# Score matmuls in two pairs per step, each into the two PSUM banks that one min pass leaves

## The chip, the core and the metric

The kernel runs on one NeuronCore of a Trainium2 chip. The metric is the device time of one execution in microseconds (us). Engines are named as the profile names them: PE (TensorE matmuls), PEld (its weight loads), DVE (VectorE), ACT (ScalarE), POOL (GpSimd), SP (the queue that issues most DMAs). Each engine takes its instructions in order and waits on semaphores for the others.

## The reference

Threshold attention over 8 batches x 8 heads x 576 positions with head size 64, followed by a hash-routed mixture of 8 experts over the 4608 resulting rows of 512. All of it is float32.

```python
scores = (1 / 8) * q @ k.T                       # per batch and head, 576 x 576
thresh = max(scores, axis=-1) - tau
scores = where(scores >= thresh, scores, -1e9)
attn   = exp(scores - max(scores)); attn /= sum(attn) + 1e-9
x      = (attn @ v), laid out as (4608, 512)
e      = token_ids * 2654435761 % 8              # the expert of each row
out    = relu(x @ w1[e]) @ w2[e]
```

## The kernel before

**Attention** takes two heads of one batch at a time, a *pair* `p`, 32 pairs in all. The 576 query rows of a head are cut into a tail of 64 and four chunks of 128. A pair is a *block* of five *steps*, `n = 5 p + s`. Step s = 0 is the tails of both heads in one 128-row tile; steps s = 1 to 4 are one 128-row chunk of each head, so they have two score tiles, head j = 0 and j = 1. One score tile is 128 rows x 576 keys in float32, which is two PSUM banks of 288 keys each (i = 0 and 1).

What a step does to a score tile, in the names used below:

- **scores** (`score`, matmuls L202 for s = 0, L209 otherwise): PE writes q k^T to PSUM. A step s >= 1 has four such calls, (i, j) = (0,0), (0,1), (1,0), (1,1). Head 0 uses rows 0 to 63 of the PE array and head 1 rows 64 to 127, so one call of each head can run side by side. Each call shows as two matmul instructions in the profile, eight in a step.
- **min pass** (`negate`, L221): DVE reads the two banks, writes the negated scores `ns` to SBUF and their row minimum `nmx`. POOL then makes the threshold `thr` from it (L225).
- **exp** (`expo`, L232): ACT makes `w = exp(-ns + nmx)`.
- **mask pass** (`mask`, L243): DVE zeroes what is under the threshold and sums the rows. It comes one step later, behind the min passes of step n + 1.
- **turn** (`turn_w`, transposes L254): two steps later PE transposes `w` into the one PSUM tile `tr` (two banks, one buffer), and ACT copies that back to SBUF (`put_wT`, L270 and L275). There are two turns per step, one per head (a tail has one). A turn can't start before the copy of the turn before it has left `tr`.
- **products** (`av_part`, L285): with the transposed weights of the pair before, PE forms w v in the tile `av`, in four parts: two for the first query columns (g = 0, steps 1 and 2) and two for the rest (g = 1, steps 3 and 4). ACT copies `av` out (L301), and in step 0 of the next block PE turns it back (`turn_o`), ACT and DVE scale it by the reciprocal sums (`put_xt` L323, `put_xm` L332) and SP writes it to DRAM.

PSUM has eight banks: two score tiles (the pool `ps_sc`, two rotating buffers of two banks), `tr` and `av`. A score tile of head j of step n + 1 takes over the buffer of the score tile two back in the rotation, so its matmuls wait for that tile's min pass; the first call of head 0 waits for one min pass and the first call of head 1, right behind it in PE's order, for the next.

The order of every engine's work is written out by hand (`manual_schedule`, the loop from L547). For PE the order of a block is:

| step | PE, in order |
|---|---|
| s = 0 | turn_o; first turn; scores of step 1; second turn |
| s = 1 | products g 0, chunks 0 to 2; first turn; scores of step 2; second turn |
| s = 2 | products g 0, chunks 3 and 4; the one turn of the tail; scores of step 3 |
| s = 3 | first turn; products g 1, chunks 0 to 2; second turn; scores of step 4 |
| s = 4 | first turn; products g 1, chunks 3 and 4; second turn; scores of the next step 0 |

DVE has per step: the min passes of step n, then (s = 0) `put_xm`, then the mask passes of step n - 1, then in early blocks a piece of the routing arithmetic, or in s = 2 a reciprocal before its min passes. ACT has in steps 1 and 2 the exp of head 0, the copy of the first turn, the exp of head 1, the copy of the second turn; in steps 3 and 4 the copy of the first turn, both exps, the copy of the second turn. At the start of step 1 POOL scales the next q tile (L182).

**The experts** follow. The router's indices are worked out during the first blocks; during the last ones rows are gathered and the first two experts' weights loaded. The first expert's first product is begun between the last steps (`early_h`, `early_xT`, L488 to L526), and the rest is a loop over the experts of `gemm1` (L651), `gemm2` (L667) and transposes. `gemm1`, `early_h`, `late_h` and `early_xT` take their PSUM from the score pool as well.

Of the kernel before, what the change touches and what calls it, by code (L numbers as in the profile page):

```python
# [20 lines left out]
def kernel(  # L21
# [17 lines left out]
    P = 128  # L39
# [31 lines left out]

    consts = ctx.enter_context(tc.tile_pool(name="consts", bufs=1))
    w_pool = ctx.enter_context(tc.tile_pool(name="w_pool", bufs=2))
    ps_sc = ctx.enter_context(tc.tile_pool(name="ps_sc", bufs=2, space=PSUM))

    ident = consts.tile([P, P], FP32, name="ident")
    u128 = consts.tile([P, P], BF16, name="u128")
# [15 lines left out]
    xT_0 = consts.tile([P, CO, CAP], FP32, name="xT_0")  # L93
    h_0 = consts.tile([P, FO, CAP], FP32, name="h_0")
    w_tiles = {}

    def gather(x_dram, dst, idx):
        nc.gpsimd.indirect_dma_start(
# [19 lines left out]
    with tc.tile_pool(name="a_q", bufs=1) as a_q, \  # L118
# [25 lines left out]

        oT = a_o.tile([P, 64 + S], FP32, name="oT")
        av = ps_av.tile([P, 2, 512], FP32, name="av")
        kts, kxs, rss, recs, scs, nss, stats, ws = {}, {}, {}, {}, {}, {}, {}, {}

        def load_pair(p):
            hp, b = divmod(p, B)  # L150
# [34 lines left out]
        def heads(n):  # L185
            return 1 if n % NS == 0 else 2

        def score(n):


            p, s = divmod(n, NS)
            q_sb, k_sb = q_bufs[p % 3], kts[p]
            for j in range(heads(n)):
                sc = ps_sc.tile([P, 2, 512], FP32, name="sc")
                scs[n, j] = sc
            if s == 0:

                for j in range(2):
                    for i in range(2):
                        rows, cols = slice(64 * i, 64 * i + 64), slice(64 * j, 64 * j + 64)  # L200
                        rhs = k_sb[rows, S2 * i:S2 * i + S2] if i == j else kxs[p][rows, :]
                        nc.tensor.matmul(scs[n, 0][cols, i, 0:S2],  # L202
                                         lhsT=q_sb[rows, TAIL + 64 * j:TAIL + 64 * j + 64],
                                         rhs=rhs, start=True, stop=True)
                return
            for i in range(2):
                for j in range(2):
                    rows, cols = slice(64 * j, 64 * j + 64), slice(P * (s - 1), P * s)
                    nc.tensor.matmul(scs[n, j][:, i, 0:S2], lhsT=q_sb[rows, cols],  # L209
                                     rhs=k_sb[rows, S2 * i:S2 * i + S2], start=True, stop=True)  # L210

        def negate(n):

            nmx = a_st.tile([P, 2], FP32, name="nmx")
            thr = a_st.tile([P, 2], FP32, name="thr")
            stats[n] = (nmx, thr)
            for j in range(heads(n)):
                sc = scs.pop((n, j))
                ns = a_ns.tile([P, S], FP32, name="ns")
                nss[n, j] = ns  # L220
                nc.vector.tensor_scalar(out=ns[:].rearrange("p (i s) -> p i s", i=2),  # L221
                                        in0=sc[:, :, 0:S2], scalar1=-1.0, scalar2=None,
                                        op0=ALU.mult, op1=ALU.min, accum_out=nmx[:, j:j + 1])
            nj = heads(n)
            nc.gpsimd.tensor_scalar(out=thr[:, 0:nj], in0=nmx[:, 0:nj], scalar1=drop[:],  # L225
                                    scalar2=None, op0=ALU.add)

        def expo(n, j):
            c0 = 64 if n % NS == 0 else S * j
# [69 lines left out]
        def put_oT(g):  # L299
            c0, width = ((64, WA), (64 + WA, WB))[g]  # L300
            nc.scalar.copy(oT[:, c0:c0 + width], av[:, g, 0:width])  # L301
# [198 lines left out]
        def early_h():  # L500

            w1_sb = w_tiles[0, 1]
            for fo in range(FO):
                h_ps = ps_sc.tile([P, 2, 512], FP32, name="sc")
                for i in range(2):
                    for co in range(CO - 1):
                        nc.tensor.matmul(h_ps[:, i, 0:CH], lhsT=w1_sb[:, co, fo * P:fo * P + P],
                                         rhs=xT_0[:, co, i * CH:i * CH + CH],
                                         start=(co == 0), stop=(co == CO - 2))
                        if (i, co) == (1, CO - 2):  # L510
                            nc.vector.tensor_copy(
                                h_0[:, fo].rearrange("p (i t) -> p i t", i=2), h_ps[:, :, 0:CH])
                        yield

        def late_h():

            w1_sb = w_tiles.pop((0, 1))
            for fo in range(FO):
                h_ps = ps_sc.tile([P, 2, 512], FP32, name="sc")
                for i in range(2):  # L520
                    nc.tensor.matmul(h_ps[:, i, 0:CH], lhsT=w1_sb[:, CO - 1, fo * P:fo * P + P],
                                     rhs=xT_0[:, CO - 1, i * CH:i * CH + CH], start=True,
                                     stop=True)
                h3 = h_0[:, fo].rearrange("p (i t) -> p i t", i=2)
                nc.vector.tensor_tensor(out=h3, in0=h3, in1=h_ps[:, :, 0:CH], op=ALU.add)
                nc.scalar.activation(h3, h3, AF.Relu)  # L526
# [12 lines left out]
        with tc.manual_schedule():  # L539
# [3 lines left out]
                nc.tensor.transpose(tr[:, 0, 0:P], ident[:], ident[:])  # L543
            next(pieces)
            scale_q(0)
            score(0)
            for n in range(LAST + NS + 1):  # L547
                p, s = divmod(n, NS)
                m = n - 2
                if s == 0 and p + 2 < NP:  # L550
                    load_pair(p + 2)
                if s == 0 and p + 1 < NP:
                    load_v(p + 1)
                if s == 1 and p + 1 < NP:
                    scale_q(p + 1)
                if s == 2 and p in (20, 24):
                    load_w1(p // 4 - 5)
                if s == 2 and p in (22, 26):
                    load_w2((p - 22) // 4)

                q = p - 1
                if s == 1 and 0 <= q < NP:
                    add_eps(q)
                if s == 2 and 0 <= q < NP:
                    nc.vector.reciprocal(recs[q][:], recs[q][:])
                if n == LAST:
                    tr = ps_sc.tile([P, 2, 512], FP32, name="sc")
                    early_xT(tr, 0, 2, 0, CO - 1)
                if s == 0 and p >= 2:
                    turn_o()  # L570
                    put_xt(p - 2)
                if n == LAST:
                    tr = ps_sc.tile([P, 2, 512], FP32, name="sc")
                    early_xT(tr, 2, 4, 0, CO - 1)
                if s in (1, 2) and 0 <= q < NP and n != LAST + 1:
                    av_part(q, 0, ((0, 1, 2), (3, 4))[s - 1])
                if n < LAST and s in (1, 2):
                    negate(n)
                    expo(n, 0)
                if s == 2 and 0 <= q < NP:  # L580
                    put_oT(0)
                if n > LAST:
                    fill(1)
                turned = 0 <= m < LAST
                if turned:
                    tr = turn_w(m, 0)
                    put_wT(m, 0, tr)
                if n == LAST:
                    tr = ps_sc.tile([P, 2, 512], FP32, name="sc")
                    early_xT(tr, 4, 5, 0, CO - 1)  # L590
                    put_xm(p - 2)
                    av_part(q, 0, (0, 1, 2))
                if n >= LAST:
                    fill(1)
                if s in (3, 4) and 0 <= q < NP:
                    av_part(q, 1, ((0, 1, 2), (3, 4))[s - 3])
                if n < LAST and s not in (1, 2):
                    negate(n)
                    expo(n, 0)
                if s == 0 and p >= 2 and n != LAST:  # L600
                    put_xm(p - 2)
                if s == 4 and 0 <= q < NP:
                    put_oT(1)
                if n < LAST and heads(n) == 2:
                    expo(n, 1)
                if s in (0, 1, 2) and n + 1 < LAST:
                    score(n + 1)
                if turned and heads(m) == 2:
                    tr = turn_w(m, 1)
                    put_wT(m, 1, tr)  # L610
                if s in (3, 4) and n + 1 < LAST:
                    score(n + 1)
                if 0 < n <= LAST:
                    for j in range(heads(n - 1)):
                        mask(n - 1, j)
                next(pieces, None)


                g = n - G0
                if 0 <= g < 2 * KT:  # L620
                    fetch(g // KT, g % KT, 0)
                if n == LAST:
                    fill(1)
# [8 lines left out]
    with tc.tile_pool(name="m_x", bufs=1) as m_x, \  # L632
# [17 lines left out]

        def gemm1(w1_sb, xT, h_sb, n, width):  # L651
            for fo in range(FO):
                h_ps = ps_sc.tile([P, 2, 512], FP32, name="sc")
                for i in range(n):
                    for co in range(CO):
                        nc.tensor.matmul(h_ps[:, i, 0:width],  # L656
# [94 lines left out]
```

## Time and profile before

| | |
|---|---|
| median of 11 runs | 1077.1 us (1073.16 to 1080.24) |
| the profiled execution | 1077.27 us, its span 1075.6 us |
| first to last min pass (attention) | 12.4 to 499.2 us from the span's start |
| last products and first expert's start | to about 535 us |
| experts, PE without a pause worth telling | from there to the end |
| granted PE clock, 100 to 500 us | 1.00 |
| busy in 100 to 500 us (400 us) | PE 390.2, PEld 259.9, DVE 373.9, ACT 340.7, POOL 137.2 us |
| one block, tail min pass to tail min pass | 15.08 to 15.09 us in 18 of the 23 blocks 8 to 30; 15.2 to 17.3 in blocks 1 to 7; 14.75 in 26 and 27 |

How to read it: all times are us from the span's start. In the timeline a row is a run of like instructions, with its start, the time from its first start to its last end, and in brackets how long the engine was idle before it and who ended that. Starts of matmuls stand closer than their durations: a run of eight score matmuls without a wait takes 1.19 to 1.20 us though each lasts 0.40 to 0.46, since two run side by side and each pair starts before the last has ended. So a PE that is busy in the table can still have been waiting. In the experts' part PE sets the pace; in the attention PE, DVE and ACT take turns at it.

### The profile page before, as it was taken

The page shows a single profiled execution, that of the slowest core. Times are in us where ns is not written, and L with a number is a line of the kernel's source. Part 1 is how long each engine was busy: PE and PEld are TensorE (multiplying, and loading weights), DVE is VectorE, ACT ScalarE, POOL GpSimd, SP SyncE. Part 2 cuts the span into 40 slices and gives each one's busy share as a digit, 9 for nine tenths or more (in the row PEclk, how much of TensorE's full clock was granted, in tenths as well). Part 3 has the DMA queues.
Part 4 walks back from the last instruction along what each step waited for, and adds up shares of the span by engine and source line. Part 5 has one row for each costly group of instructions (what it writes and reads, how often), then busy time and mean ns, then how long its engine had stood idle before and what let it go on. Part 6 is the DMA issues. An engine that isn't in the chain of part 4 may idle for free. (4 is left out here: it accounts for less than half of the span.)

```text
span 1075.6 us, 20177 instructions
## 1 busy us (share of the span) xinstructions
PE 1043.8 (97%) x7438; PEld 650.9 (61%) x7438; DVE 522.9 (49%) x1347; ACT 469.1 (44%) x798; POOL 299.5 (28%) x397
## 2 busy tenths in 40 slices
PE   7999999999999999999999999999999999999996
PEld 5666666666666666666655746557466475564652
DVE  8898899999999999996330100100101001010000
ACT  5788888888888888887020000010000000000000
POOL 2566632222222225422433114022140140101001
PEclk8899999999999999999999999999999999999998
DMA  4332343333335656411133124212242042300000
GB/s 118 93 97 67 97 103 87 84 90 104 97 89 156 177 177 203 124 46 30 36 132 113 53 89 143 87 59 96 96 147 85 30 131 95 103 0 35 9 18 27
DMA packets 95460, 97.40 MB, mean 91 GB/s; under 512 B 33275, under 2 KB 70269, under 8 KB 95362
## 3 DMA queue, kind: packets, MB, share of 16 engines
q1 hardware_dynamic: 87170, 77.20, 24.6%
q0 software_dynamic: 8192, 18.91, 5.2%
q8 instruction: 60, 0.98, 0.4%
q14 instruction: 38, 0.31, 0.1%
HBM read 78.18 MB, written 19.98 MB: 91 GB/s over the span
## 5 line engine op out<-in xcount | busy, mean ns | idle before, releaser
L670 PE MATMUL o_ps<-w_sb,h 128*122 128x512 f32 x640 | 280.6, 592 | 0.0
L232 ACT ACTIVATE w<-ns,nmx 128x576 f32<-128x576 f32 x288 | 220.4, 777 | 35.8 <-DVE ns L221 34.0
L243 DVE SCALAR_TENSOR_TENSOR w<-ns,thr,w 128x576 f32<-128x576 f32 x288 | 232.7, 840 | 0.0
L656 PE MATMUL sc<-xT,w_sb 128*128 128x305 f32 x896 | 231.2, 419 | 0.0
L221 DVE TENSOR_SCALAR_CACHE_REDUCE ns<-sc 128x576 f32<-128x576 f32 x288 | 207.2, 752 | 23.9 <-PE sc L209 22.3
L656 PEld LDWEIGHTS sc<-xT,w_sb 128*128 128x128 f32 x896 | 169.1, 189 | 63.4 <-issue 3.4
L670 PEld LDWEIGHTS o_ps<-w_sb,h 128*122 128x122 f32 x640 | 115.6, 185 | 138.9 <-issue 138.5
L209 PE MATMUL sc<-k_sb,q 64*128 64x288 f32 x1024 | 181.3, 429 | 1.5 <-DVE ns L221 1.5
L254 PEld LDWEIGHTS tr<-ident,w 64*128 64x128 f32 x2624 | 123.1, 139 | 91.4 <-ACT wT_a L275 39.0
L254 PE MATMUL tr<-ident,w 64*128 64x64 f32 x2624 | 158.1, 232 | 13.3 <-ACT wT_a L275 13.3
L225 POOL TENSOR_SCALAR thr<-nmx,drop 128x2 f32<-128x2 f32 (+1 forms) x160 | 99.5, 622 | 229.5 <-DVE ns L221 225.2
L674 POOL DMA_INDIRECT out_dram<-o,gidx x40 | 39.7, 991 | 415.1 <-ACT o L673 401.5
L673 ACT COPY o<-o_ps 122x512 f32<-122x512 f32 x40 | 23.4, 585 | 293.5 <-PE o_ps L670 293.5
L664 DVE TENSOR_SCALAR h<-sc 128x610 f32<-128x610 f32 x28 | 22.2, 793 | 256.9 <-PE sc L656 256.9
L209 PEld LDWEIGHTS sc<-k_sb,q 64*128 64x128 f32 x1024 | 110.4, 192 | 21.9 <-DVE ns L221 9.4
L649 DVE COPY xT<-xT_ps 128x488 f32<-128x488 f32 x35 | 23.2, 664 | 183.4 <-PE xT_ps L647 183.4
L285 PE MATMUL av<-wT_a,v 128*64 128x320 f32 (+1 forms) x704 | 101.7, 422 | 0.8 <-DVE xm L332 0.8
L662 ACT ACTIVATE h<-sc 128x610 f32<-128x610 f32 x28 | 19.0, 679 | 182.7 <-PE sc L656 182.7
L275 ACT COPY wT_b<-tr 128x512 f32<-128x512 f32 (+1 forms) x128 | 81.3, 635 | 27.4 <-PE tr L254 23.6
L275 ACT COPY wT_a<-tr 128x512 f32<-128x512 f32 (+1 forms) x128 | 81.6, 637 | 20.2 <-PE tr L254 19.7
L285 PE MATMUL av<-wT_b,v 128*64 128x256 f32 x640 | 83.2, 389 | 0.0
L285 PEld LDWEIGHTS av<-wT_a,v 128*64 128x64 f32 x704 | 44.2, 138 | 30.1 <-issue 1.2
(100 smaller groups left out, 587.8 us busy)
## 6 DMA issues: line engine op xcount, KB each, us to landing
w_sb<-in_moe_w_dram SPq DMA_DIRECT2D x16, 2048.0 KB
q<-in_q_dram SPq DMA_DIRECT2D x32, 256.0 KB
v<-in_v_dram SPq DMA_DIRECT2D x32, 256.0 KB
xa_scratch<-xm SPq DMA_DIRECT2D x24, 256.0 KB
k_sb<-in_k_dram SPq DMA_DIRECT2D x32, 144.0 KB
k_sb<-in_k_dram SPq DMA_DIRECT2D x32, 128.0 KB
kx<-in_k_dram SPq DMA_DIRECT2D x32, 72.0 KB
q<-in_q_dram SPq DMA_DIRECT2D x64, 32.0 KB
```

The lines of the kernel that those rows point to most:

```text
L209: nc.tensor.matmul(scs[n, j][:, i, 0:S2], lhsT=q_sb[rows, cols], rhs=k_sb[rows, S2 * i:S2 * i + S2], start=True, stop=True)
L221: nc.vector.tensor_scalar(out=ns[:].rearrange("p (i s) -> p i s", i=2), in0=sc[:, :, 0:S2], scalar1=-1.0, scalar2=None, op0=ALU.mult, op1= ...
L225: nc.gpsimd.tensor_scalar(out=thr[:, 0:nj], in0=nmx[:, 0:nj], scalar1=drop[:], scalar2=None, op0=ALU.add)
L232: nc.scalar.activation(w, nss[n, j][:], AF.Exp, bias=stats[n][0][:, j:j + 1], scale=-1.0)
L243: nc.vector.scalar_tensor_tensor(out=w, in0=nss.pop((n, j))[:], scalar=stats[n][1][:, j:j + 1], in1=w, op0=ALU.is_le, op1=ALU.mult, accum_ ...
L254: nc.tensor.transpose(dst[:, r, 64 * c:64 * c + 64], src[rows, c0:c0 + P], ident[rows, rows])
L275: nc.scalar.copy(dst, tr[:, :, 0:64 * n_c].rearrange("p r (c q) -> p r c q", c=n_c))
L285: nc.tensor.matmul(av[64 * j:64 * j + 64, g, c0:c1], lhsT=v_sb[:, c, 64 * j:64 * j + 64], rhs=wT[g][:, i, c0:c1], start=(c == 0), stop=stop)
L656: nc.tensor.matmul(h_ps[:, i, 0:width], lhsT=w1_sb[:, co, fo * P:fo * P + P], rhs=xT[:, co, i * width:i * width + width], start=(co == 0), ...
L670: nc.tensor.matmul(o_ps[0:rows], lhsT=h_sb[:, fo, kt * rows:kt * rows + rows], rhs=w2_sb[:, fo, :], start=(fo == 0), stop=(fo == FO - 1))
L673: nc.scalar.copy(o_sb[0:rows], o_ps[0:rows])
L674: nc.gpsimd.indirect_dma_start(out=out[:, :], out_offset=bass.IndirectOffsetOnAxis(ap=idx, axis=0), in_=o_sb[:], in_offset=None, bounds_ch ...
```

## The change

The four banks of the score pool become one tile `sc` of four banks, allocated once. Which bank holds what is worked out per step by `sc_banks`: `use[i][j]` is the bank of the matmul of pair i and head j, `own[j]` the two banks of head j. The two matmuls of pair i of step n + 1 (head 0 and head 1, side by side) go into the two banks that *one* min pass of step n leaves. So the layout of a head alternates: banks (0,2) and (1,3) in steps 1 and 3, (0,1) and (2,3) in steps 2 and 4. In step 1, pair 0 goes into banks 2 and 3, which the second min pass of step 4 left, and pair 1 into 0 and 1, which the tail's min pass leaves. The min pass reads its two banks with a stride of one or two banks. A head still needs one matmul of each pair.

`score` and `negate` are called once per pair and per head. The first pair of step n + 1 is issued between the two min passes of step n, the second behind the second min pass; in step 0 the first pair of step 1 is issued ahead of the first turn, the second behind the tail's min pass. On PE the order within steps 1 to 4 is the same as before; in step 0 it becomes: turn_o; first pair of step 1; first turn; second pair; second turn. The order on DVE, ACT and POOL stays. The experts' PSUM tiles are the two halves of `sc` in turn.

```diff
-    ps_sc = ctx.enter_context(tc.tile_pool(name="ps_sc", bufs=2, space=PSUM))
+    ps_sc = ctx.enter_context(tc.tile_pool(name="ps_sc", bufs=1, space=PSUM))
+    sc = ps_sc.tile([P, 4, 512], FP32, name="sc")
...
+    def half_sc():
+        i = 2 * (half_count[0] % 2)
+        half_count[0] += 1
+        return sc[:, i:i + 2]
...
+        def sc_banks(n):
+            if n not in banks:
+                s = n % NS
+                if n == 0:
+                    use = ((0, 1), (2, 3))
+                elif s == 1:
+                    use = sc_banks(n - 1)[0][::-1]
+                else:
+                    use = sc_banks(n - 1)[1]
+                own = tuple(tuple(sorted(pair)) for pair in zip(*use))
+                banks[n] = (use, own if s else use)
+            return banks[n]
...
-            for i in range(2):
-                for j in range(2):
-                    rows, cols = slice(64 * j, 64 * j + 64), slice(P * (s - 1), P * s)
-                    nc.tensor.matmul(scs[n, j][:, i, 0:S2], lhsT=q_sb[rows, cols],
-                                     rhs=k_sb[rows, S2 * i:S2 * i + S2], start=True, stop=True)
...
+            for j in range(2):
+                rows, cols = slice(64 * j, 64 * j + 64), slice(P * (s - 1), P * s)
+                keys = S2 * own[j].index(use[i][j])
+                nc.tensor.matmul(sc[:, use[i][j], 0:S2], lhsT=q_sb[rows, cols],
+                                 rhs=k_sb[rows, keys:keys + S2], start=True, stop=True)
...
+        def negate(n, j):
...
+            i0, i1 = sc_banks(n)[1][j]
...
+            nc.vector.tensor_scalar(out=ns[:].rearrange("p (i s) -> p i s", i=2),
+                                    in0=sc[:, i0:i1 + 1:i1 - i0, 0:S2], scalar1=-1.0,
+                                    scalar2=None, op0=ALU.mult, op1=ALU.min,
+                                    accum_out=stats[n][0][:, j:j + 1])
...
+                if s == 0 and n + 1 < LAST:
+                    score(n + 1, 0)
                 if turned:
                     tr = turn_w(m, 0)
                     put_wT(m, 0, tr)
...
+                if s in (3, 4) and turned:
+                    tr = turn_w(m, 1)
+                if s != 0 and n + 1 < LAST:
+                    score(n + 1, 0)
                 if n < LAST and heads(n) == 2:
+                    negate(n, 1)
                     expo(n, 1)
-                if s in (0, 1, 2) and n + 1 < LAST:
-                    score(n + 1)
-                if turned and heads(m) == 2:
+                if s in (3, 4) and turned:
+                    put_wT(m, 1, tr)
+                if n + 1 < LAST:
+                    score(n + 1, 1)
+                if s in (0, 1) and turned:
                     tr = turn_w(m, 1)
                     put_wT(m, 1, tr)
-                if s in (3, 4) and n + 1 < LAST:
-                    score(n + 1)
```

## The prediction

> **What bounds the kernel now.** First the page's table of busy time and its costliest groups, then the list of waits in 100 to 500 us, then the timeline of one block. The page:
>
> ```profile
> PE 1043.8 (97%) x7438; PEld 650.9 (61%) x7438; DVE 522.9 (49%) x1347; ACT 469.1 (44%) x798; POOL 299.5 (28%) x397
> L221 DVE TENSOR_SCALAR_CACHE_REDUCE ns<-sc 128x576 f32<-128x576 f32 x288 | 207.2, 752 | 23.9 <-PE sc L209 22.3
> L209 PE MATMUL sc<-k_sb,q 64*128 64x288 f32 x1024 | 181.3, 429 | 1.5 <-DVE ns L221 1.5
> ```
>
> Shares of the span mix two halves. From 520 us on PE runs without a pause and no score matmul is left; what the change is worth is decided in the attention. There DVE is busy 373.9 of 400 us and its only real idle time stands before min passes that wait for scores, 22.3 us in all. PE seems to wait for a min pass for 1.5 us alone. The waits say more, since the weight loads (PEld) stop where PE's order stops (columns: total, times, longest, us):
>
> ```profile
> PEld tr L254 <- ACT wT_a L275: 30.5, 80, 0.5
> DVE ns L221 <- PE sc L209: 20.3, 53, 0.6
> PEld sc L209 <- DVE ns L221: 5.6, 25, 0.7
> ```
>
> 25 waits of scores for a min pass are about one a block, and 80 of a turn for the copy before it about three a block. Where in the block they are, and which of them reaches the end, the timeline shows (block 19, tail min pass at 305.20):
>
> ```profile
> 305.53 0.46 PE L254 MATMUL tr<-ident,w 64*128 64x64 f32 x8 [0.36 <-ACT wT_a L275]
> 305.83 1.42 PE L209 MATMUL sc<-k_sb,q 64*128 64x288 f32 x8
> 306.86 0.69 PE L254 MATMUL tr<-ident,w 64*128 64x64 f32 x10
> 307.48 1.83 PE L285 MATMUL av<-wT_a,v 128*64 128x320 f32 x12
> ...
> 309.25 0.47 PE L254 MATMUL tr<-ident,w 64*128 64x64 f32 x8
> 309.26 0.78 ACT L232 ACTIVATE w<-ns,nmx 128x576 f32<-128x576 f32 x1 [0.92 <-DVE ns L221]
> 309.55 1.40 PE L209 MATMUL sc<-k_sb,q 64*128 64x288 f32 x7
> 309.94 0.56 ACT L275 COPY wT_b<-tr 128x512 f32<-128x512 f32 x1
> 309.95 0.78 PEld L209 LDWEIGHTS sc<-k_sb,q 64*128 64x128 f32 x6 [0.17 <-DVE ns L221]
> ...
> 310.79 0.40 PE L209 MATMUL sc<-k_sb,q 64*128 64x288 f32 x1
> 310.80 0.70 PE L254 MATMUL tr<-ident,w 64*128 64x64 f32 x7
> 311.43 1.30 PE L285 MATMUL av<-wT_a,v 128*64 128x320 f32 x10
> ...
> 312.66 0.53 PE L254 MATMUL tr<-ident,w 64*128 64x64 f32 x10
> ...
> 313.02 1.20 PE L209 MATMUL sc<-k_sb,q 64*128 64x288 f32 x8
> ...
> 314.24 0.76 DVE L221 TENSOR_SCALAR_CACHE_REDUCE ns<-sc 128x576 f32<-128x576 f32 x1 [0.55 <-PE sc L209]
> ```
>
> The reader is to see this. In step 2 the eight score matmuls take 1.20 us (313.02): nothing holds them. In step 1 they go from 309.55 to 311.19, because only head 0's first call may start; head 1's waits for the second min pass (weights from 309.95), and the two halves of the array then run out of step. The second turn of step 1 is dragged along (310.57 to 311.50 where such a turn takes 0.53), then everything behind it on PE: products 311.43, the tail's turn 312.66, scores of step 3 at 313.02. DVE stands idle 0.55 us for these before step 3's min pass. A further 0.28 us is lost before step 4's (317.45); from 313.02 PE has run in order without a hole to there, 3.2 us from the scores of step 3 (313.02) to those of step 4 (316.22). Between step 4's min pass and the min passes of the next step 1 DVE has no wait. So a block's length is a loop: DVE to the min pass of step 1, the exp and copy behind it on ACT, the second turn, then PE alone to step 4's scores, then DVE again. PE's waits for the min passes lie in it although PE seems busy.
>
> [...]
>
> **The change, part by part.** All starts are of block 19.
>
> *Step 1, two pairs.* Both matmuls of the first pair need the first min pass alone, which ends at 309.22 (308.47 + 0.75), so they run at 309.55 side by side; the second pair needs the second min pass, which ends 309.90 (309.15 + 0.75). A pair is half of the 1.03 us that scores without a wait take from their start to the next instruction's (313.02 to 314.04): the first ends its issue at 310.07, the second at 310.57. The second turn needs the copy that ends at 310.50 (309.94 + 0.56) and starts at 310.57 as now, but alone on PE: 0.53 instead of 0.93 us. Its end is 311.10 instead of 311.50, and the products come 0.41 earlier (311.02). Next in line: its copy on ACT starts at 311.19, behind the exp of head 1 that leaves ACT about 311.1, and ends 311.9; the tail's turn needs `tr` at 312.25, so it is not held. Scores of step 3 at 312.61, their min pass at 313.83. DVE is ready at 313.69 (idle 0.55 up to 314.24), so 0.14 of the 0.55 stays. Gain 0.41.
>
> *Step 0, first pair ahead of the first turn.* PE is idle before that turn (0.36 above) while the copy before it runs; turn_o's last transpose starts about 304.95, `tr` comes free at 305.48. A pair of 0.52 fits, 305.02 to 305.54, with the turn at 305.55 instead of 305.53. It waits for nothing: its banks were left by step 4's second min pass (303.04 + 0.75). Price if that cover were gone: 0.5 us a block. The second pair starts at 306.02, behind the tail's min pass (305.95), and ends 306.55; the second turn needs the copy 306.09 to 306.68 and takes 306.74 to 307.27 instead of 306.86 to 307.55. Products of step 1 come 0.28 earlier, and so does its first turn; its copy, though, waits on ACT for the exp behind the first min pass (309.22), which is DVE's time. Worth in this block: 0. In blocks 26, 27 and 31 POOL's scaling of q doesn't stretch a mask pass (1.15 us at 306.65, others 0.81); step 1's min pass comes 0.35 earlier and PE is the one behind (waits of 0.34, 0.21 and 0.28 us, length 14.75). There the 0.28 counts, together with the scores' stretch of 1.31 instead of 1.20; the second turn then waits for its copy (ends 416.21 - 0.2), about 0.38 in all.
>
> *Steps 2, 3, 4.* Same order on PE; scores of step 3 and 4 run in 1.20 and 1.19 us now, so no wait is there to be removed. The second pair's wait for the second min pass is over before PE gets there: 312.21 against 312.61, 315.27 against 315.8. The 0.28 before step 4 stays: it is PE's 3.2 us against DVE's 2.85. The tail's scores keep their place; the second min pass of step 4 is emitted behind them but shares no bank. Worth 0.
>
> *Layout and emission.* Same instructions in the same numbers: no DMA, no POOL instruction, no matmul more. DVE's order is unchanged, so a min pass for head 1 delays no mask pass unless it gets a new wait. A stride of two banks instead of one in the min pass: the trace has no such read; bounds are 0 (the same 576 elements, row of 752 ns) and, upwards, a second start like the 81 ns that the accumulator read adds, 4 passes a block, 0.3 us. I take 0, as element count is the same; 0.3 is kept for the range (4 x 0.081 x 24 blocks = 8 us). The experts' tiles alternate between two halves as between two buffers: 0.
>
> *The sum.* Blocks 1 to 7 have steps 1 and 2 stretched by POOL's scatters and routing, PE has slack there, and step 4's remaining 0.2 comes behind ACT's copy: 0. Blocks 8 to 31 are 24: 21 x 0.41 + 3 x 0.38 = 9.8 us. Nothing behind the attention starts earlier or later by itself: the experts move up as a whole. 1077.27 - 9.8 = 1067.5 for the profiled execution, which stands 0.2 above the median; 1067 for the median.
>
> **The rivals.**
>
> *A. More: DVE becomes the bound.* If PE gains enough that both waits vanish: 0.55 + 0.28 = 0.83 x 24 = 20 us, 1057. For it: step 0's 0.28 is spare. Against: the turn of step 1 hangs on ACT's copy at 310.50, whatever PE gained.
>
> *B. Nothing: another wait takes the place.* If the copy of step 1's second turn starts no earlier, because ACT gets to it no sooner than now (311.59), the tail's turn waits for `tr` until 312.3: that costs nothing yet. It would take 0.4 more on ACT. Or the two halves of the array stay out of step for another reason. Gain 0 to 3 us: 1074 to 1077.
>
> *C. Slower: a wait that isn't in the data.* All four banks are one tile now, and a min pass that steps over a bank spans it. If the program's dependencies are drawn over the span, head 1's min pass (banks 1, 3) waits for the first pair of the next step, which writes bank 2 just ahead of it in the order. In step 1 that pair is done at about 309.97, so the pass moves from 309.15 by 0.82; in step 3 it lies behind 1.5 us of products and the second turn and is done at about 316.5 where the pass is due at 314.52: 2.0. Both mask passes and the next min passes queue behind it on DVE, POOL's threshold and the next exp behind them. 2.8 less 0.41 and less the idle 0.28 that it covers is 2.1 x 32 = 67 us: 1144. It decides from 0.41 a block on, so step 1's alone is enough. Against it: today's exp of head 0 starts at 309.26, straight behind the first min pass, though the second pass writes the next column of the same `nmx` tile: orders follow columns there. No strided case is in the trace.
>
> **How the numbers follow.** Forecast 0.63 (own range 1062 to 1072), A 0.08, B 0.16, C 0.13. Below 1060 is most of A, above 1076 are C and the last of B: 1060 to 1076 holds about 0.8; the 8 us of a dearer strided read lie in it. A change of 0.2% (2.1 us) is about what this kernel's runs can tell from none. Faster: forecast, A and two thirds of B, 0.81; same: the rest of B, 0.06; slower: C.
>
> **What would show it.** Right: a block of 14.68 us; all eight scores of step 2, issued in step 1, within 1.2 us; the wait before step 3's min pass down from 0.55 to about 0.14 and the one before step 4's still 0.28; a pair of scores ahead of step 0's first turn and no 0.36 there. Wrong: a DVE wait before head 1's min passes in steps 1 and 3 (C), a min pass over 752 ns, or turns of step 1 that still start products at 311.43 after the tail's pass at 305.20, that is 6.23 into the block (B).

## The result, and the profile after

The changed kernel takes 1338.3 us (median of 8 runs, 1336.9 to 1339.4) against 1077.2 us for the kernel before beside it: a ratio of 1.242, interval 1.2405 to 1.2437. It is 261 us slower where 10 us of gain were forecast.

The page of the kernel after, busy time and the costliest groups (busy us, mean ns of one | idle us before them, and what ended most of it):

```profile
PE 1120.8 (84%) x7438; PEld 625.3 (47%) x7438; DVE 529.0 (39%) x1347; ACT 485.5 (36%) x798; POOL 306.8 (23%) x397
L248 DVE TENSOR_SCALAR_CACHE_REDUCE ns<-sc 128x576 f32<-128x576 f32 x288 | 216.9, 753 | 231.0 <-PE sc L237 158.0
L237 PE MATMUL sc<-k_sb,q 64*128 64x288 f32 x1024 | 197.3, 463 | 111.0 <-DVE ns L248 110.3
L693 PE MATMUL sc<-xT,w_sb 128*128 128x305 f32 x896 | 244.3, 425 | 41.6 <-ACT h L699 21.5
```

The work is the same: 288 min passes, 1024 score matmuls, 896 matmuls of the experts' first layer. A min pass still takes 753 ns (752 before), so the strided read costs nothing. What grew is the idle time. DVE stands 231.0 us before min passes (23.9 before the change), PE 111.0 us before scores (1.5) and 41.6 us before the experts' first layer, where it had none. The waits of 200 to 600 us, all inside the attention, show that both engines wait for each other (us in total, times, longest):

```profile
DVE ns L248 <- PE sc L237: 87.7, 55, 2.7
PE sc L237 <- DVE ns L248: 62.2, 93, 0.9
DVE ns L248 <- PE sc L230: 44.2, 19, 3.3
```

Where in a block that is, the timeline of block 18 tells (start, length; in brackets the idle time before; its tail min pass starts at 403.47):

```profile
407.55 0.76 PE L237 MATMUL sc<-k_sb,q 64*128 64x288 f32 x4
408.36 0.76 DVE L248 TENSOR_SCALAR_CACHE_REDUCE ns<-sc 128x576 f32<-128x576 f32 x1 [0.86 <-PE sc L237]
409.18 0.76 PE L237 MATMUL sc<-k_sb,q 64*128 64x288 f32 x4 [0.87 <-DVE ns L248]
...
411.76 0.70 PE L237 MATMUL sc<-k_sb,q 64*128 64x288 f32 x4
...
412.51 0.76 DVE L248 TENSOR_SCALAR_CACHE_REDUCE ns<-sc 128x576 f32<-128x576 f32 x1 [1.77 <-PE sc L237]
413.33 0.76 PE L237 MATMUL sc<-k_sb,q 64*128 64x288 f32 x4 [0.87 <-DVE ns L248]
...
416.36 0.70 PE L237 MATMUL sc<-k_sb,q 64*128 64x288 f32 x4
...
417.12 0.76 DVE L248 TENSOR_SCALAR_CACHE_REDUCE ns<-sc 128x576 f32<-128x576 f32 x1 [1.68 <-PE sc L237]
417.94 0.76 PE L237 MATMUL sc<-k_sb,q 64*128 64x288 f32 x4 [0.88 <-DVE ns L248]
...
422.05 0.76 DVE L248 TENSOR_SCALAR_CACHE_REDUCE ns<-sc 128x576 f32<-128x576 f32 x1 [2.01 <-PE sc L230]
```

In steps 1 to 3, head 1's min pass (the DVE rows) starts only when the four matmuls issued just ahead of it are done: in step 1, 407.55 + 0.76 = 408.31, and the pass starts at 408.36; in step 2, 412.46 and 412.51; in step 3, 417.06 and 417.12. Those matmuls are the first pair of the *next* step and write other banks than the pass reads. The second pair then waits for that min pass, which it would have to do anyway. The pass of step 4 waits in the same way for the scores of the next tail (L230).

The four waits are 0.86 + 1.77 + 1.68 + 2.01 = 6.32 us. They swallow the old 0.55 and 0.28 and a wait of 0.09 before `put_xm`'s pass, and the mask pass beside POOL's scaling of q takes 1.32 instead of 1.15: 6.32 - 0.92 + 0.17 = 5.57. The block went from 15.08 to 20.74, which is 5.66, so 0.09 stays unexplained.

The experts have a wait of their own. The waits from 735 us to the end; before the change there was none of this kind:

```profile
PE sc L693 <- ACT h L699: 21.5, 28, 0.8
PE sc L693 <- DVE h L701: 20.1, 21, 1.0
```

A group of the first layer writes one half of the score tile while ACT or DVE reads the other half, and PE waits for that reader.

The whole difference of the two profiled executions, 1342.1 - 1075.6 = 266.5 us of span, is then: blocks 0 to 7 48.0; blocks 8 to 30 146.8 (23 x 5.66 = 130, and about 17 for a slower PE clock, below); block 31 3.6; what follows the last min pass 66.9 (644.1 against 577.2); the start 1.2.

### The profile page after: what moved, and what is told of

It is laid out like the page before. It is cut to its first block, busy times and chain, and to the rows that moved or that the text cites. A ratio compares the mean times of both kernels' runs of the same rounds, so it can differ in the third digit from the quotient of the medians.

```text
span 1342.1 us, 20217 instructions
## 1 busy us (share of the span) xinstructions
PE 1120.8 (84%) x7438; PEld 625.3 (47%) x7438; DVE 529.0 (39%) x1347; ACT 485.5 (36%) x798; POOL 306.8 (23%) x397
## 5 line engine op out<-in xcount | busy, mean ns | idle before, releaser
L248 DVE TENSOR_SCALAR_CACHE_REDUCE ns<-sc 128x576 f32<-128x576 f32 x288 | 216.9, 753 | 231.0 <-PE sc L237 158.0
L237 PE MATMUL sc<-k_sb,q 64*128 64x288 f32 x1024 | 197.3, 463 | 111.0 <-DVE ns L248 110.3
L693 PE MATMUL sc<-xT,w_sb 128*128 128x305 f32 x896 | 244.3, 425 | 41.6 <-ACT h L699 21.5
L693 PEld LDWEIGHTS sc<-xT,w_sb 128*128 128x128 f32 x896 | 165.3, 189 | 121.9 <-ACT h L699 35.1
L284 PEld LDWEIGHTS tr<-ident,w 64*128 64x128 f32 x2624 | 115.8, 144 | 153.0 <-ACT wT_a L305 80.0
L284 PE MATMUL tr<-ident,w 64*128 64x64 f32 x2624 | 146.2, 238 | 42.3 <-ACT wT_a L305 39.2
L237 PEld LDWEIGHTS sc<-k_sb,q 64*128 64x128 f32 x1024 | 80.3, 192 | 170.2 <-DVE ns L248 169.3
L315 PE MATMUL av<-wT_a,v 128*64 128x320 f32 (+1 forms) x704 | 112.7, 458 | 0.0
L315 PE MATMUL av<-wT_b,v 128*64 128x256 f32 x640 | 86.8, 402 | 0.0
L315 PEld LDWEIGHTS av<-wT_a,v 128*64 128x64 f32 x704 | 48.2, 150 | 35.4 <-issue 11.5
```

The source lines that it names most:

```text
L237: nc.tensor.matmul(sc[:, use[i][j], 0:S2], lhsT=q_sb[rows, cols], rhs=k_sb[rows, keys:keys + S2], start=True, stop=True)
L284: nc.tensor.transpose(dst[:, r, 64 * c:64 * c + 64], src[rows, c0:c0 + P], ident[rows, rows])
L315: nc.tensor.matmul(av[64 * j:64 * j + 64, g, c0:c1], lhsT=v_sb[:, c, 64 * j:64 * j + 64], rhs=wT[g][:, i, c0:c1], start=(c == 0), stop=stop)
L693: nc.tensor.matmul(h_ps[:, i, 0:width], lhsT=w1_sb[:, co, fo * P:fo * P + P], rhs=xT[:, co, i * width:i * width + width], start=(co == 0), ...
```

## The experiments

The theory after the result: the program orders all accesses to a PSUM tile by the tile and not by the bank. A read waits for the last write that was emitted to any bank of the tile, a write for the last read of any bank. The list of waits in the built program of the changed kernel says so for a min pass of head 1 in step 2 (offsets in elements; the tile is [P, 4, 512], 512 to a bank):

```
DVE L248 min pass   reads sc, offset 1024 and 1536 (banks 2, 3)
     waits for      PE L237 matmul into sc, offset 512 (bank 1), the one emitted just ahead of it
```

Nothing is stepped over there, so this is not the span of rival C. That makes three suspects to be taken apart on the chip: the one tile, the layout with its strides, and the order in which scores and min passes are emitted. The runs were made in three sets, each beside its own runs of the kernel before (1078.3, 1090.8 and 1077.7 us), so ratios are compared.

### The tile alone

The kernel before, with its two score buffers made the halves of one tile; orders of work, layout and emission as before.

```diff
-    ps_sc = ctx.enter_context(tc.tile_pool(name="ps_sc", bufs=2, space=PSUM))
+    ps_sc = ctx.enter_context(tc.tile_pool(name="ps_sc", bufs=1, space=PSUM))
+    sc_all = ps_sc.tile([P, 4, 512], FP32, name="sc")
...
-                sc = ps_sc.tile([P, 2, 512], FP32, name="sc")
+                sc = half_sc()
...
-                h_ps = ps_sc.tile([P, 2, 512], FP32, name="sc")
+                h_ps = half_sc()
```

> The kernel before with nothing changed but the allocation: its two rotating score buffers become two halves of one tile of four banks. Theory (every read of a PSUM tile is ordered behind the last write to any part of it, and every write behind the last read of any part): the experts lose what they lost with the change, since each group of their first product must wait until the other half is read; 607.0 - 540.6 = 66 us behind 735 and 535 us. In the attention all scores of a step wait for its second min pass, which costs at most what the pairs side by side give back, 0 +- 8 us. Total 1143 us (1135 to 1152). Rival (the new order of the attention's work alone is to blame, the tile is innocent): 1077 us.

Measured: 1149.4 us, 1.0659 of before (1.0636 to 1.0683). The group of the experts' first layer on its page:

```profile
L664 PE MATMUL sc<-xT,w_sb 128*128 128x305 f32 x896 | 244.3, 425 | 41.6 <-ACT h L670 21.5
```

That is the changed kernel's row to the tenth. What follows the last min pass takes 643.8 us against 577.2: 66.6 of the 71 us. The attention is only 4.9 us longer (most of it in blocks 0 to 7; the later ones are 15.11), since in the old emission both min passes of a step come ahead of the next scores. So one tile alone costs the experts their two buffers, with no change of layout. The rival, that halves of a tile are as good as two buffers, falls.

### The experts given buffers of their own

The changed kernel, with the loop's first layer taking PSUM from a pool of two buffers; the four-bank tile is given up behind the attention.

```diff
+         tc.tile_pool(name="ps_h", bufs=2, space=PSUM) as ps_h, \
...
-                h_ps = half_sc()
+                h_ps = ps_h.tile([P, 2, 512], FP32, name="h_ps")
```

> The changed kernel, whose experts take their first product's PSUM from two rotating tiles of two banks again. Theory (order over the whole tile): the experts' 66 us come back and nothing else, 1338 - 66 = 1272 us (1262 to 1282); blocks of the attention still 20.5 to 22.1 us. Rival (the experts are slow for another reason, the clock or late data): 1338 us.

Measured: 1282.4 us, 1.1893 (1.1863 to 1.1923), 57 us less than the changed kernel by the ratio, and 10 above what was expected. The row of the loop's first layer:

```profile
L696 PE MATMUL h_ps<-xT,w_sb 128*128 128x305 f32 x896 | 231.2, 419 | 0.0
```

In the loop the idle time is gone, and the matmul's mean is back from 425 to 419 ns. What follows the last min pass is 591.0 us, 13.8 above the kernel before: the first expert's first layer (`early_h`, `late_h`) still uses the halves of the tile, and the weight loads wait 8.8 and 6.5 us for DVE there, which my expectation had left out. The blocks are those of the changed kernel (20.73 and 22.08), so the attention's loss is another matter.

### Emission: both min passes ahead of the first pair

The changed kernel with its tile, layouts and strides; each step's min passes are emitted before the next step's first pair.

```diff
                 if n < LAST and s in (1, 2):
                     negate(n, 0)
+                    negate(n, 1)
                     expo(n, 0)
...
+                if s == 0 and n < LAST:
+                    negate(n, 0)
                 if s == 0 and n + 1 < LAST:
                     score(n + 1, 0)
...
                 if n < LAST and s not in (1, 2):
-                    negate(n, 0)
+                    if s > 0:
+                        negate(n, 0)
+                        negate(n, 1)
                     expo(n, 0)
...
                 if n < LAST and heads(n) == 2:
-                    negate(n, 1)
                     expo(n, 1)
```

> The changed kernel with its layouts and strided reads, but both min passes of a step stand ahead of the first pair in the program's order (in step 0 the one min pass), so that no min pass has a later write to the tile ahead of it. Theory: the waits of min passes for scores (0.86 to 3.3 us each, four a block) go. In step 0 the first pair now waits for the tail's pass and holds the first turn up to 1 us, some 0.3 a block. Blocks 15.1 to 15.6 us, experts still 66 us slower: 1150 us (1140 to 1165). Rival (the alternating layout, or reading banks with a stride, is slow in itself): blocks stay above 20 us, 1300 us or more.

Measured: 1157.2 us, 1.0732 (1.0700 to 1.0764). The blocks are 15.36 instead of 20.74, and no min pass of head 1 waits at all. Beside 0.09 before step 3's first min pass and the old 0.28 before step 4's, what is left in a block stands before the first min pass of step 2:

```profile
302.56 0.76 DVE L248 TENSOR_SCALAR_CACHE_REDUCE ns<-sc 128x576 f32<-128x576 f32 x1 [0.74 <-PE sc L237]
```

Now both pairs wait for the later min pass, so step 1 is 0.28 worse than before the change and nothing of the split is left. The layout with its strides is the changed kernel's, so neither is what made it slow: the order of emission is, under orders by tile. The rest of the 1.0732 is the experts again (644.3 us behind the last min pass).

### Orders by bank, as a control

The kernel before, with a switch of the program builder. What it changes shows in block 19 of the kernel with both parts, below: with it head 1's min pass of step 1 (305.65, 0.74 us) runs beside the pair emitted ahead of it (305.78), which writes other banks of the tile; without it the pass waits 0.86 us for that pair.

```diff
+import os
+os.environ["TILE_EXHAUSTIVE_MEMORY_SHARE_CHECK"] = "1"
```

> The kernel before, built with the framework's switch that has it work out exactly which bytes of a tile two accesses share. Control for the runs that need the switch. Theory: its PSUM tiles hold one thing at a time, so hardly a wait changes: 1077 us, within 0.3%. If the coarse rule already cost the kernel before something, it is faster: down to 1067 us, and then this is what later runs must be compared with.

Measured: 1077.4 us, 0.9995 (0.9985 to 1.0006). The kernel before loses nothing to orders by tile, so what the switch gives to another kernel is that kernel's own wait.

### Both parts of the change, with orders by bank

The two parts that the prediction priced (two pairs in step 1; the first pair ahead in step 0), with the switch. The layout is one in which no min pass steps over a bank that is being written: banks (0,2) and (1,3) in step 2 only, whose two min passes come ahead of the next scores. In steps 2, 3 and 4 all scores of the next step come behind both min passes, so step 1 alone is split. The changed kernel's own layout with orders by bank was not tried, because its min passes step over a bank that PE writes at that time; whether that is free stays open. The edit against the changed kernel:

```diff
+os.environ["TILE_EXHAUSTIVE_MEMORY_SHARE_CHECK"] = "1"
...
+        USE = (((1, 2), (0, 3)),
+               ((0, 3), (1, 2)),
+               ((0, 1), (2, 3)),
+               ((0, 3), (1, 2)),
+               ((0, 3), (1, 2)))
...
                     negate(n, 0)
+                    if s == 2:
+                        negate(n, 1)
                     expo(n, 0)
...
                     negate(n, 0)
+                    if s > 2:
+                        negate(n, 1)
                     expo(n, 0)
...
-                if s != 0 and n + 1 < LAST:
+                if s == 1 and n + 1 < LAST:
                     score(n + 1, 0)
                 if n < LAST and heads(n) == 2:
-                    negate(n, 1)
+                    if s == 1:
+                        negate(n, 1)
                     expo(n, 1)
...
                 if n + 1 < LAST:
+                    if s > 1:
+                        score(n + 1, 0)
                     score(n + 1, 1)
```

> What the change is after, with waits per byte range instead of per tile: built with the exact switch; the layout is chosen so that no strided read spans a bank that is being written (tail in banks 1,2; pairs of step 1 in 0,3 and 1,2; of step 2, issued in step 1, in 0,1 and 2,3, each left by one min pass; steps 3 and 4 issued behind both min passes as before). Has both parts that the prediction priced. Theory (the prediction's sum holds once the tile-wide orders are gone): blocks of 14.68 instead of 15.08 us, the wait before step 3's min pass 0.14 instead of 0.55, before step 4's still 0.28; 1067 us (1062 to 1072). Rival (another wait takes the place: the copies of step 1's second turn start no earlier): 1074 to 1077 us.

Measured: 1080.7 us against 1090.8, 0.9907 (0.9884 to 0.9929). The prediction was 1067.0 of 1077.1, which is 0.9906. Its timeline, block 19 (tail min pass at 301.69):

```profile
301.50 0.70 PE L238 MATMUL sc<-k_sb,q 64*128 64x288 f32 x4
...
302.04 0.45 PE L285 MATMUL tr<-ident,w 64*128 64x64 f32 x8
...
305.78 1.43 PE L238 MATMUL sc<-k_sb,q 64*128 64x288 f32 x8
...
306.45 0.30 PEld L238 LDWEIGHTS sc<-k_sb,q 64*128 64x128 f32 x4 [0.38 <-DVE ns L249]
...
307.06 0.52 PE L285 MATMUL tr<-ident,w 64*128 64x64 f32 x10
...
307.51 1.30 PE L316 MATMUL av<-wT_a,v 128*64 128x320 f32 x10
...
308.74 0.52 PE L285 MATMUL tr<-ident,w 64*128 64x64 f32 x10
...
309.10 1.19 PE L238 MATMUL sc<-k_sb,q 64*128 64x288 f32 x8
...
310.32 0.76 DVE L249 TENSOR_SCALAR_CACHE_REDUCE ns<-sc 128x576 f32<-128x576 f32 x1 [0.16 <-PE sc L238]
...
313.52 0.76 DVE L249 TENSOR_SCALAR_CACHE_REDUCE ns<-sc 128x576 f32<-128x576 f32 x1 [0.28 <-PE sc L238]
```

Counted from the tail's min pass, the second turn starts at 5.37, the products at 5.82, the tail's turn at 7.05, the scores of step 3 at 7.41 and their min pass at 8.63. The prediction's starts, counted in the same way from 305.20, are 5.37, 5.82, 7.05, 7.41 and 8.63. The block is 14.68, the wait 0.16 where 0.14 was predicted, the other still 0.28.

### Each part alone

Both from the kernel above. Without step 0's part:

```diff
-                if s == 0 and n + 1 < LAST:
-                    score(n + 1, 0)
...
-                    if s > 1:
+                    if s != 1:
                         score(n + 1, 0)
```

> The one before, with step 0 as in the kernel before (both pairs of step 1 behind the first turn). Only step 1's split is left. Theory: the same blocks of 14.68 us where POOL's scaling stretches a mask pass (21 of 24), a little longer in the other three: 1068 us (1063 to 1073). Rival (the first pair in step 0's hole is what pays): 1074 to 1077 us.

Without step 1's part (its two min passes ahead of all scores):

```diff
-               ((0, 1), (2, 3)),
+               ((0, 3), (1, 2)),
...
                     negate(n, 0)
-                    if s == 2:
-                        negate(n, 1)
+                    negate(n, 1)
...
-                if s == 1 and n + 1 < LAST:
-                    score(n + 1, 0)
...
-                    if s == 1:
-                        negate(n, 1)
                     expo(n, 1)
...
-                    if s > 1:
+                    if s > 0:
                         score(n + 1, 0)
```

> The one before the last, with step 1 as in the kernel before (first call of each head waits for its own min pass); only step 0's first pair ahead of the first turn is left. Theory: blocks stay 15.08 us except the three without the stretched mask pass, 1076 us (1074 to 1078). Rival (PE's earlier products in step 1 reach the end after all): 1065 to 1072 us.

Measured: step 1's part alone 0.9909 (0.9887 to 0.9931) with blocks of 14.68; step 0's alone 0.9994 (0.9979 to 1.0009) with blocks mostly of 15.08 to 15.10 and the old 0.55 before step 3's min pass. The gain is the split in step 1, and step 0's pair is worth nothing that can be measured, as the prediction's steps had it.

### Step 4's scores earlier, for the 0.28

From the kernel with both parts; in step 3 the scores of step 4 go ahead of the second turn.

```diff
+                if s == 3 and n + 1 < LAST:
+                    score(n + 1, 0)
+                    score(n + 1, 1)
                 if s in (3, 4) and turned:
                     tr = turn_w(m, 1)
...
                 if n + 1 < LAST:
-                    if s > 1:
+                    if s in (2, 4):
                         score(n + 1, 0)
-                    score(n + 1, 1)
+                    if s != 3:
+                        score(n + 1, 1)
```

> The first of these four with, in step 3, the scores of step 4 ahead of the second turn instead of behind it. Aimed at the 0.28 us wait before step 4's min pass, which the prediction left alone. Theory (PE's order alone makes that wait, and steps 4 and 0 have room for the later turn): blocks of 14.4 us, 1060 us (1055 to 1066). Rival (the later turn holds the first turn of step 4 through the one buffer, and products behind it): 1067 us or more.

Measured: 1.0125 (1.0102 to 1.0147), a miss; blocks of 15.36. The 0.28 before step 4's min pass is gone, but step 4's first turn and the tail's min pass have new waits:

```profile
311.78 0.46 PE L285 MATMUL tr<-ident,w 64*128 64x64 f32 x8 [0.84 <-ACT wT_a L306]
...
314.49 0.76 DVE L249 TENSOR_SCALAR_CACHE_REDUCE ns<-sc 128x576 f32<-128x576 f32 x1 [0.91 <-PE sc L231]
```

The second turn of step 3 now comes behind the scores, its copy on ACT ends later, and the next turn waits for the one tile `tr`. The scores of the tail stand behind that turn. My expectation had moved a turn without following who waits for its copy.

### The switch taken away again

The kernel with both parts, without the two lines of the switch.

```diff
-import os
-os.environ["TILE_EXHAUSTIVE_MEMORY_SHARE_CHECK"] = "1"
```

> The kernel with both parts of the change and orders by bank (0.9907 of before), this time with one order for the whole of the tile. It tells whether that order alone turns the change's gain into a loss. If it does: step 1's min pass of head 1 waits for the first pair, about 0.9 us a block, the tail's min pass waits for the first pair ahead of it, about 0.6, the pairs of step 1 and step 2 wait for the later min pass, about 0.5 to 1 more, and the experts' first layer adds 56 to 66 us as in the kernel with one tile: 32 x 2 + 60 us, so 1.10 of before (1.06 to 1.16). If the order does not matter: 0.991 again (0.988 to 0.994).

Measured: 1181.6 us, 1.0969 (1.0953 to 1.0986). One source, two orders of its accesses: 0.9907 and 1.0969. Its timeline, block 19:

```profile
324.06 0.76 DVE L247 TENSOR_SCALAR_CACHE_REDUCE ns<-sc 128x576 f32<-128x576 f32 x1 [0.62 <-PE sc L236]
...
328.15 0.76 PE L236 MATMUL sc<-k_sb,q 64*128 64x288 f32 x4
...
328.95 0.76 DVE L247 TENSOR_SCALAR_CACHE_REDUCE ns<-sc 128x576 f32<-128x576 f32 x1 [0.86 <-PE sc L236]
```

The 0.86 of the changed kernel's step 1 is back, and the tail's min pass waits 0.62 for the first pair ahead of it. With the mask pass at 1.32 instead of 1.15, 0.06 less before step 3 and 0.09 less before `put_xm`'s pass, that is 1.50 of the 1.60 between blocks of 14.68 and 16.28; 646.0 us behind the last min pass are the experts' share. This shows that the order alone turns the gain into a loss.

### What is late next: POOL's scaling of q

With the split in place DVE has no wait in steps 0 to 2, but its first mask pass there is long. In the kernel with both parts:

```profile
302.89 0.80 POOL L192 TENSOR_SCALAR q<-q,keep_any 128x640 f32<-128x640 f32 x1
...
303.15 1.15 DVE L274 SCALAR_TENSOR_TENSOR w<-ns,thr,w 128x576 f32<-128x576 f32 x1
```

The same kernel with two statements swapped, so that POOL scales q after the factors' addition and beside the min passes:

```diff
-                if s == 1 and p + 1 < NP:
-                    scale_q(p + 1)
...
                     add_eps(q)
+                if s == 1 and p + 1 < NP:
+                    scale_q(p + 1)
```

> The same kernel with the scaling of q on POOL emitted after the factors' addition in step 1. It tells what is late next after the change: in the kernel with both parts and orders by bank the mask pass beside the scaling takes 1.15 us where its neighbours take 0.81. If DVE's own passes are now the bound in that step, the block loses that 0.34: 14.68 to 14.34 us, 21 x 0.34 = 7.1 us, so 0.9907 - 0.0066 = 0.984 of before (0.980 to 0.988). The rival: the scaling stretches another pass of DVE by as much, or PE's products and turns are late next: 0.991 again (0.988 to 0.994).

Measured: 1060.6 us against 1077.7, 0.9831 (0.9809 to 0.9853): faster than the kernel before and than the changed one. Block 19 of it:

```profile
299.55 0.81 DVE L274 SCALAR_TENSOR_TENSOR w<-ns,thr,w 128x576 f32<-128x576 f32 x1
...
301.62 0.80 POOL L192 TENSOR_SCALAR q<-q,keep_any 128x640 f32<-128x640 f32 x1
...
301.70 0.75 DVE L249 TENSOR_SCALAR_CACHE_REDUCE ns<-sc 128x576 f32<-128x576 f32 x1
```

The mask pass is 0.81, the min pass beside the scaling keeps its 0.75, and the block is 14.34, 0.34 less. So POOL's scaling stretched the mask pass that ran beside it (1.15 us against 0.81) and doesn't stretch the min pass. The mask pass reads two SBUF tiles and the min pass one PSUM tile; whether that makes the difference no run here shows.

## Why the prediction was wrong

**The step that failed** is *Layout and emission*, taken at 0. Its sentence that a min pass for head 1 delays no mask pass "unless it gets a new wait" named the case, and the wait was there in all four steps of 32 blocks: 6.32 us a block where 0 was put. Its last sentence, that the experts' tiles alternate between two halves as between two buffers, failed for the same reason: 66.9 us behind the last min pass where 0 was put.

**Rival C** had the right kind of wait and the wrong extent. Step 1's wait was priced at 0.82 and measured 0.86, step 3's at 2.0 and measured 1.68. That the first two are so near is luck: the price was 0.40 until the pair starts and 0.42 for the pair, while on the chip the pair starts 0.05 after the pass could have and takes 0.76. It gave steps 2 and 4 none, since their banks aren't spanned, and they cost 1.77 and 2.01; and it did not reach the experts. So it said 67 us where the chip showed 261. The argument against it was that `nmx`, a tile in SBUF, is followed by its columns. That was true and didn't carry over: the built program orders the score tile in PSUM as a whole. No row of the kernel before shows two engines at two banks of one PSUM tile at once, so its trace could not decide; 0.13 was too little for a case that no row excluded.

**Step 1, two pairs**: right, in mechanism and in size, once the orders go by bank (0.41 predicted, 0.40 from blocks of 15.08 to 14.68). That the totals agree to 0.9906 and 0.9907 is partly luck. By the profiled executions, which are of different sets, blocks 8 to 30 are 7.8 us shorter (346.8 to 339.0) where the sum has 9.4 for them: block 26 gains 0.08 where 0.38 was put, and block 27 is 0.79 longer, whose cause stays open. Blocks 0 to 7 are 1.0 longer instead of the same. One sign was off: the eight scores take 1.43 us, not 1.2, because the first pair starts early and the second waits for the second min pass; the second turn, which waits for its copy, starts at the same time.

**Step 0, first pair ahead**: worth 0 as predicted; in blocks 26, 27 and 31, where 0.28 of it was to count, the kernels with and without it differ by 0.07 at most. **Steps 2, 3, 4**: their pairs were not tested with orders by bank, since those kernels keep all scores behind both min passes there; the 0.28 before step 4 stayed in them. DVE's side of that wait is 2.93 by the rows (317.45 - 0.28 - 314.24), not 2.85. **The strided read**: 753 against 752 ns, so the 8 us kept for it in the range weren't needed.

**Rival A** (1057) asked for both waits to vanish. They didn't; the next gain came from DVE's own mask pass instead, 0.34 a block. PE's matmul row looks like a cap before the change: it leaves 9.8 of 400 us free, 11.9 of the 487 us of attention. It is none: in the kernel with the scaling moved the attention, first to last min pass, takes 470.0 us against 486.1, which is 16.1 less. **Rival B** asked for ACT's copy of the second turn to come no sooner; with orders by bank it came with its turn, and no other wait took the place.

What stays open: the changed kernel's own layout, with its pairs in steps 2 to 4, under orders by bank, as said above.

## What to carry to other kernels

Before merging buffers into one tile, find out by what the program orders accesses: buffers that two engines use at the same time belong in separate PSUM tiles, or need orders by bank, however disjoint the data is (here one source took 0.9907 of before with orders by bank and 1.0969 with orders by tile). A sum over moved work holds only if the waits of the new program are those of the data, so read the waits of the built program where the trace has no case of that kind. After a wait is removed, look at the passes of the engine that is now late for a neighbour that stretches them: here moving one POOL instruction brought some 8 us beside the 10 of the change's own idea.

## What the chip showed that was not expected

The changed kernel's blocks have two lengths, 20.47 to 20.75 us, and 21.8 to 22.1 in 13 of the 23 blocks 8 to 30. In the longer ones PE was granted half its clock for a stretch of 3.4 us (in the one below 0.50 in every half microsecond from 398.50 to 401.50). The stretches of time around one such, from the end of block 17 (us, then busy us of PE, PEld, DVE, ACT and POOL, the granted clock, DMA share, GB/s), and the tail's scores in it and a block later at full clock:

```profile
390.00:395.00 5.00, 4.06 (x42) 2.06 (x40) 2.92 (x8) 3.03 (x5) 0.73 (x1) 1.00 0.00 2
395.00:400.00 5.00, 3.51 (x36) 1.88 (x37) 2.92 (x8) 2.98 (x5) 0.72 (x1) 0.82 0.19 43
400.00:403.50 3.50, 2.58 (x22) 1.12 (x22) 2.19 (x7) 1.39 (x3) 0.72 (x1) 0.77 0.69 191
403.50:410.00 6.50, 5.27 (x58) 3.18 (x60) 5.64 (x17) 4.54 (x8) 2.04 (x4) 1.00 0.33 78
```

```profile
399.93 0.74 PE L230 MATMUL sc<-k_sb,q 64*64 64x288 f32 x1
...
421.19 0.45 PE L230 MATMUL sc<-k_sb,q 64*64 64x288 f32 x1
```

Each costs about 1.3 us, 13 x 1.3 = 17 us of the 261. PE has no pause over 0.88 us there. The kernel with both parts and without the switch has pauses of up to 0.87 us too and shows a clock of 1.00 from 200 to 460 us; but PE is busy 90% of that time (235.4 of 260 us) and 78% in the changed kernel (311.8 of 400). So it isn't the longest pause alone; whether the share of busy time decides is not shown, since no run here varied it alone.
